# Later weight and input loads, one VectorE operation per tile for the block-diagonal keys, and retuned scheduling constants, in a two-layer sliding-window attention kernel

## The chip, the cores and the metric

The kernel runs on one core of a Trainium2 chip. The metric is the device time of the slowest core in microseconds, here simply of the one core. Executions of one kernel lie up to 1% or a little more apart (the kernel before took 368.29 to 371.98 us), so differences of 1% need several rounds. A run that is over 1.5% above the fastest of its kernel counts as slow; ratios leave it out. A ratio below is the mean time of one kernel's fast runs over that of the other's in the same rounds, so it is not quite the ratio of the medians that are quoted beside it. The kernel before stands at medians of 369.5 to 370.4 us, depending on the chip. A profile is one execution; its span is some 2 us shorter than the time.

## The reference

Two layers, with the same weights in both. In each, attention with a window of 256 over 2048 rows (32 heads of 16), and then a small MLP for the single row whose router value is highest:

```python
q, k, v = heads(layernorm(x) @ wqkv)                  # S = 2048, D = 512, H = 32, Dh = 16
scores = einsum("bhqd,bhkd->bhqk", q, k) * Dh ** -0.5
mask = (i - j >= 0) & (i - j < 256)
x = x + merge(softmax(where(mask, scores, -1e9)) @ v) @ wo
r = layernorm(x) @ w_r                                 # router; one row is chosen
y = (silu(x_sel @ w_gate) * (x_sel @ w_up)) @ w_down * sigmoid(r_sel)
x = layernorm(x) + scatter(y)
# ... both parts once more
```

## The kernel before

A program in Python lists every instruction of 32 tiles (16 of 128 rows, two layers) with its dependencies, an estimated duration and a priority. A list scheduler simulates the engines with those durations and from that fixes the order on each engine and the semaphores. So an instruction's estimated duration and a handful of priority constants decide the order of all the others. Each engine then works through its own list in that order (in `x8_late`, below, one instruction of VectorE's waits for 9.50 us, and everything behind it stands).

A tile's keys go from PSUM to `KTN`, and from there, block-diagonally for four heads, to `KT`: for each of four heads a multiplication by a 0/1 column of `KM`.

```python
def pk(MB=banks[1]):                                   # keys of one tile
    S.prio_base = p0 + self.P_K * 1e6 if L or m else -7e6
    ...                                                # 16 matmuls into the shared PSUM bank
    S.add("dve", lambda e: e.tensor_copy(out=self.KTN[:, k2], in_=...), dur=690, name="evk", tr=t)
    S.prio_base += self.P_KBD * 1e6 if L or m else 0.0
    for hh in range(4):
        S.add("dve", lambda e, hh=hh: e.tensor_scalar(
            out=self.KT[:, k4, :, :, hh, :].rearrange("p s b k -> p (s b) k"),
            in0=self.KTN[:, k2].rearrange("p s (b k) -> p (s b) k", k=32),
            scalar1=self.KM[:, hh:hh + 1], scalar2=None, op0=ALU.mult), dur=470, name="kbd", ...)
```

The query eviction to `QT` comes behind these on VectorE, and the output projection of the tile before waits for it, as keys, queries, values and output projection take turns in one PSUM bank.

A tile's values go from VectorE (`VN`) to DRAM (`vscr`) and come back spread out as `VBD` in four loads; only then can the product of probabilities and values (PV) run. GpSimd multiplies the probabilities by a mask (128x384), and makes the layer-norm of a tile two ahead: from VectorE's aggregate (`MV`) through a power (the reciprocal root) to `XN`. `XN` and the attention output `OT` are transposed by DMA. V writes, V loads, transposes and x loads are issued in one queue, SyncE's.

```python
ldx(0, 1, ...); ldw(1, ...); ldw(0, ...); ldx(1, 2, ...); ldw(2, ...)       # first two x tiles, wqkv
self.late_loads = [ldx(2, 4), lwo, lwr, ldx(4, 8), ldx(8, 16)]               # all after the first statistics
```

## Time and profile before

| | |
|---|---|
| time, median of 3 (lowest, highest) | 369.74 us (369.0, 370.61) |
| span of the profile, granted clock | 368.4 us, 0.969 |
| TensorE, VectorE, ScalarE, GpSimd busy | 92, 76, 73, 67% |

The rows of the page are read as: engine, operation, output<-inputs, shape, count, busy time and mean ns of one, idle time ahead of it.

### The profile page before, as it was taken

The page shows a single profiled execution, that of the slowest core. Times are in us where ns is not written, and L with a number is a line of the kernel's source. Part 1 is how long each engine was busy: PE and PEld are TensorE (multiplying, and loading weights), DVE is VectorE, ACT ScalarE, POOL GpSimd, SP SyncE. Part 2 cuts the span into 40 slices and gives each one's busy share as a digit, 9 for nine tenths or more (in the row PEclk, how much of TensorE's full clock was granted, in tenths as well). Part 3 has the DMA queues.
Part 4 walks back from the last instruction along what each step waited for, and adds up shares of the span by engine and source line. Part 5 has one row for each costly group of instructions (what it writes and reads, how often), then busy time and mean ns, then how long its engine had stood idle before and what let it go on. Part 6 is the DMA issues. An engine that isn't in the chain of part 4 may idle for free.

```text
span 368.4 us, 17614 instructions
## 1 busy us (share of the span) xinstructions
PE 339.3 (92%) x7770; PEld 274.3 (74%) x7770; DVE 281.0 (76%) x702; ACT 270.5 (73%) x296; POOL 245.5 (67%) x457
## 2 busy tenths in 40 slices
PE   8868889999999999999888998999999999999993
PEld 3566767888888888888677677877777788888771
DVE  7947768878888778777884597997787777786870
ACT  6559667888888888899191697779888888889600
POOL 4477758787877877766490479987776676566530
PEclk9969999999999999999997899999999999999986
DMA  8643524565555443363322123433232343322110
GB/s 261 229 73 63 115 63 113 134 123 124 104 102 103 84 118 93 88 99 91 89 59 21 30 48 78 60 64 74 52 72 61 77 77 76 77 58 56 27 32 25
DMA packets 72725, 31.25 MB, mean 85 GB/s; under 512 B 52672, under 2 KB 72000, under 8 KB 72640
## 3 DMA queue, kind: packets, MB, share of 16 engines
q1 hardware_dynamic: 70384, 27.81, 35.3%
q10 hardware_dynamic: 2256, 2.23, 1.9%
q8 instruction: 63, 1.03, 1.2%
q14 instruction: 22, 0.18, 0.2%
HBM read 14.29 MB, written 7.87 MB: 60 GB/s over the span
## 4 chain that ended last, share of the span: by engine, by line
PE 60%; DVE 21%; POOL 6%; DMA 5%; ACT 4%; issue 2%; DVEq 0%; POOLq 0%
PE f_PS L1331 16%; PE f_PS L1292 13%; PE f_PS L790 11%; PE f_PS L857 8%; DVE f_KT L816 8%; PE f_PS L826 6%; ACT f_PT L1301 4%; DMA f_OT<-f_ONORM 3%; POOL f_PT L1307 3%; DVE f_KTN L812 2%; DVE f_QT L1146 2%; PE f_PS L1010 2%; DMA f_XNT<-f_XN 1%; PE f_PS L1352 1%; DVE f_ST L744 1%
## 5 line engine op out<-in xcount | busy, mean ns | idle before, releaser
L1301 ACT ACTIVATE f_PT<-f_PS 128x1024 bf16<-128x1024 f32 x276 | 260.6, 1027 | 67.0 <-PE f_PS L1292 39.8
L1307 POOL TENSOR_TENSOR f_PT<-f_PT,f_TM 128x384 bf16<-128x384 bf16 x128 | 117.9, 922 | 39.1 <-ACT f_PT L1301 37.3
L1331 PEld LDWEIGHTS f_PS<-f_VBD,f_PT 128*128 128x128 bf16 x2880 | 106.2, 98 | 22.7 <-DVE f_ONORM L844 5.4
L1331 PE MATMUL f_PS<-f_VBD,f_PT 128*128 128x68 bf16 x2880 | 115.4, 197 | 5.2 <-POOL f_MV L748 2.8
L1292 PE MATMUL f_PS<-f_QT,f_KT 64*128 64x128 bf16 (+3 forms) x2976 | 90.2, 203 | 2.8 <-ACT f_PT L1301 2.4
L1292 PEld LDWEIGHTS f_PS<-f_QT,f_KT 64*128 64x128 bf16 x2976 | 70.4, 94 | 15.9 <-ACT f_PT L1301 5.5
L790 PE MATMUL f_PS<-f_XNT,f_wqkv 128*128 128x128 bf16 x1024 | 69.9, 223 | 2.3 <-DVE f_VN L829 0.9
L790 PEld LDWEIGHTS f_PS<-f_XNT,f_wqkv 128*128 128x128 bf16 x1024 | 59.8, 100 | 6.1 <-DVE f_VN L829 1.0
L816 DVE TENSOR_SCALAR f_KT<-f_KTN,f_KM 128x512 bf16<-128x512 bf16 x128 | 60.1, 529 | 1.0
L857 PE MATMUL f_PS<-f_wo,f_OT 128*128 128x512 bf16 x128 | 33.6, 384 | 9.5 <-DVE f_QT L1146 5.1
L812 DVE CAST f_KTN<-f_PS 128x512 bf16<-128x512 f32 x32 | 22.1, 690 | 26.0 <-PE f_PS L790 26.0
L880 POOL TENSOR_SCALAR f_RSM<-f_xres 128x1 f32<-128x1 f32 x32 | 7.6, 239 | 46.5 <-DVE f_xres L874 45.4
L826 PE MATMUL f_PS<-f_wqkv,f_XNT 128*128 128x512 bf16 x128 | 33.4, 381 | 0.8 <-DVE f_QT L1146 0.8
L844 DVE TENSOR_TENSOR f_ONORM<-f_PS,f_RDA 128x256 bf16<-128x256 f32 x64 | 27.0, 422 | 1.8
L875 DVE SCALAR_TENSOR_TENSOR f_JUNK<-f_xres,f_WR 128x512 bf16<-128x512 f32 x32 | 25.1, 784 | 0.1
L857 PEld LDWEIGHTS f_PS<-f_wo,f_OT 128*128 128x128 bf16 x128 | 10.1, 96 | 19.6 <-issue 6.9
L1290 PE MATMUL f_PS<-f_BM,f_II 64*128 64x64 bf16 (+1 forms) x256 | 24.6, 189 | 0.0
L829 DVE CAST f_VN<-f_PS 128x512 bf16<-128x512 f32 x32 | 22.1, 690 | 3.0 <-PE f_PS L826 2.5
L842 DVE RECIPROCAL f_RDA<-f_PS 128x16 f32<-128x16 f32 x64 | 16.1, 251 | 10.3 <-PE f_PS L1331 9.9
L1146 DVE CAST f_QT<-f_PS 128x512 bf16<-128x512 f32 x31 | 21.1, 681 | 3.5 <-PE f_PS L790 3.4
L873 DVE BATCH_NORM_STATS2 f_ST<-f_xres 128x6 f32<-128x512 f32 x32 | 22.2, 692 | 1.0
L882 POOL TENSOR_TENSOR f_xres<-f_RSM,f_MHALF 128x1 f32<-128x1 f32 x32 | 17.8, 555 | 6.8 <-DVE f_DOT L878 3.7
(133 smaller groups left out, 286.2 us busy)
## 6 DMA issues: line engine op xcount, KB each, us to landing
f_vscr<-f_VN SPq DMA_DIRECT2D x32, 136.0 KB, 2.0
f_VBD<-f_vscr SPq DMA_DIRECT2D x128, 34.0 KB, 2.4
out_dram<-f_OUTB SPq DMA_DIRECT2D x16, 128.0 KB, 2.6
f_xin<-in_B_w_down_dram SPq DMA_DIRECT2D x14, 128.0 KB, 2.1
f_wg<-in_B_w_gate_dram SPq DMA_DIRECT2D x7, 256.0 KB, 3.7
f_wu<-in_B_w_up_dram SPq DMA_DIRECT2D x7, 256.0 KB, 3.9
f_wqkv<-in_A_wqkv_dram ACTq DMA_DIRECT2D x3, 512.0 KB, 5.7
f_xscr<-f_xres SPq DMA_DIRECT2D x5, 256.0 KB, 2.3
```

The costliest lines, as they stand in the source:

```text
L790: r = e.matmul(self.bank(MB)[:, 128 * s:128 * s + 128], lhsT=self.wqkv[:, kc, off:off + 128], rhs=self.XNT[:, k2, kc, :], start=(kc == 0), ...
L812: S.add("dve", lambda e: e.tensor_copy(out=self.KTN[:, k2], in_=self.bank(MB)[:, 0:512].rearrange("p (s t) -> p s t", s=4)), reads=[], wri ...
L816: S.add("dve", lambda e, hh=hh: e.tensor_scalar(out=self.KT[:, k4, :, :, hh, :].rearrange("p s b k -> p (s b) k"), in0=self.KTN[:, k2].rea ...
L826: return e.matmul(self.bank(MB)[:, 0:512], lhsT=self.XNT[:, k2, kc, :], rhs=self.wqkv[:, kc, 1024:1536], start=(kc == 0), stop=(kc == 3))
L844: S.add("dve", lambda e: e.tensor_tensor(out=self.ONORM[:, ko, 256 * half:256 * half + 256].rearrange("p (h d) -> p h d", d=16), in0=acc[: ...
L857: return e.matmul(self.bank(MB)[:, 0:512], lhsT=self.OT[:, ko, kc, :], rhs=self.wo[:, kc, :], start=(kc == 0), stop=(kc == 3))
L875: S.add(D, lambda e: e.scalar_tensor_tensor(out=self.JUNK[:], in0=x, scalar=1.0, in1=self.WR16[:], op0=ALU.mult, op1=ALU.mult, accum_out=s ...
L1146: self.S.add("dve", lambda e: e.tensor_copy(out=self.QT[:, k2], in_=self.bank(MB)[:, 0:512].rearrange("p (s t) -> p s t", s=4)), reads=[], ...
L1292: r = e.matmul(o, lhsT=self.KT[p, (b // 4) % 4, s, b % 4].rearrange("p h k -> p (h k)"), rhs=self.QT[p, k2, s, q:q + w], start=(i == 0), s ...
L1301: S.add("act", lambda e: e.activation(out=view, in_=self.PS[:, b0:b0 + 2, 0:128 * nu].rearrange("p h (u c) -> p h u c", u=nu), func=ACTF.E ...
L1307: S.add("pool", lambda e: e.tensor_tensor(out=w, in0=w, in1=self.TM[:].unsqueeze(1).broadcast_to([128, k, 2, 32]), op=ALU.mult), reads=["t ...
L1331: r = e.matmul(self.bank(BK_PV)[:, c0:c0 + 68], lhsT=self.PT[:, w1:w1 + 128], rhs=self.VBD[:, (b // 4) % 4, b % 4].rearrange("p h (g c) -> ...
```

## The change

Its intent: keep the DMA engines free for the first tiles by sending the loads that are needed later, later; and write the four heads' keys by one instruction with a mask tensor, so that VectorE does less. The scheduler's constants were tuned again with it.

```diff
-        self.late_loads = [lambda d: ldx(2, 4, ...), lambda d: ldx(4, 8, ...), lambda d: ldx(8, 16, ...)]
+        self.late_loads = [(0, "st6_0", lambda d: ldx(2, 4, ...)), (0, "vn0", lambda d: ldx(4, 8, ...)),
+                           (1, "vn1", lambda d: ldx(8, 16, ...))]          # vn0, vn1: eviction of the first, second V tile
+        self.late_loads += [(0, "xnt0", lwo), (0, "vn0", lwr)]              # w_r now on SyncE's queue
...
-            for hh in range(4):
-                S.add("dve", lambda e, hh=hh: e.tensor_scalar(... scalar1=self.KM[:, hh:hh + 1] ...), dur=470, name="kbd")
+            S.add("dve", lambda e: e.tensor_tensor(
+                out=self.KT[:, k4].rearrange("p s b h k -> p (s b) h k"),
+                in0=self.KTN[:, k2].rearrange(...).unsqueeze(2).broadcast_to([128, 16, 4, 32]),
+                in1=self.KMB[:].unsqueeze(1).broadcast_to([128, 16, 4, 32]), op=ALU.mult), dur=1450, name="kbd")
...
-    P_Q = -0.321;  P_K = -0.417;  P_V = 0.232;  P_STEP = 1.112;  P_NORM = -0.33;   P_LEAD = 730.15
+    P_Q = -0.343;  P_K = -0.361;  P_V = 0.129;  P_STEP = 1.169;  P_NORM = -0.838;  P_LEAD = 456.083
     # cut: P_SP, P_PVJ, P_KBD, P_LN, P_FIN, P_MG, P_PV likewise
```

Below, **D** is the loads, **K** the key operation and **C** the constants. D also moves two small VectorE operations on w_r (`init_late`) behind the first tile's projections.

More of the change, by code (lines that the diff above doesn't have):

```diff
@@ L630, in alloc @@
         self.KM = self.sb("KM", [128, 4], F32)
+        self.KMB = self.sb("KMB", [128, 4, 32], BF16)
         self.IDXI = self.sb("IDXI", [128, NT], I32)
@@ L686, in init @@
         ldw(2, -8.7e9)
-        self.late_loads = [lambda d: ldx(2, 4, "sp", -8.6e9, d), lambda d: ldx(4, 8, "sp", -8.3e9, d), lambda d: ldx(8, 16, "sp", -8.2e9, d)]
+        self.late_loads = [(0, "st6_0", lambda d: ldx(2, 4, "sp", -8.6e9, d)), (0, "vn0", lambda d: ldx(4, 8, "sp", -4.9e6, d)),
+                           (1, "vn1", lambda d: ldx(8, 16, "sp", -4.7e6, d))]
         def lwo(d):
             S.dma("act", lambda e: e.dma_start(self.wo[:], self.A_wo.rearrange("(kc p) n -> p kc n", p=128)),
-                  writes=["wo"], nbytes=1440000, name="ld_wo", dur=650, prio=-8.5e9, extra_deps=d)
+                  writes=["wo"], nbytes=1440000, name="ld_wo", dur=650, prio=-6.8e6, extra_deps=d)
         def lwr(d):
-            S.dma("act", lambda e: e.dma_start(self.WR16[:], self.B_w_r.partition_broadcast(128)),
-                  writes=["wr16"], nbytes=1540000, name="ld_wr", dur=650, prio=-8.4e9, extra_deps=d)
-        self.late_loads.insert(1, lwo)
-        self.late_loads.insert(2, lwr)
+            S.dma("sp", lambda e: e.dma_start(self.WR16[:], self.B_w_r.partition_broadcast(128)),
+                  writes=["wr16"], nbytes=1540000, name="ld_wr", dur=650, prio=-4.8e6, extra_deps=d)
+        self.late_loads += [(0, "xnt0", lwo), (0, "vn0", lwr)]
         S.add(P, lambda e: e.memset(self.MHALF[:], -0.5), writes=["mhalf"], dur=100, prio=-9.5e9)
@@ L714, in init @@
                   reads=["kf2"], writes=["km%d" % hh], dur=150)
+        S.add(D, lambda e: e.tensor_copy(out=self.KMB[:], in_=self.KM[:].unsqueeze(2).broadcast_to([128, 4, 32])), reads=["km%d" % hh for hh in range(4)], writes=["kmb"], dur=200)
         S.add(P, lambda e: e.memset(self.ONESF[:], 1.0), writes=["onesf"], dur=200, prio=-8.1e9)
@@ L814, in pk @@
             S.prio_base += self.P_KBD * 1e6 if L or m else 0.0
-            for hh in range(4):
-                S.add("dve", lambda e, hh=hh: e.tensor_scalar(
-                    out=self.KT[:, k4, :, :, hh, :].rearrange("p s b k -> p (s b) k"),
-                    in0=self.KTN[:, k2].rearrange("p s (b k) -> p (s b) k", k=32), scalar1=self.KM[:, hh:hh + 1], scalar2=None, op0=ALU.mult),
-                    reads=["ktn%d" % k2, "km%d" % hh], writes=["kt%d_%d" % (k4, hh)], dur=470, name="kbd")
+            S.add("dve", lambda e: e.tensor_tensor(
+                out=self.KT[:, k4].rearrange("p s b h k -> p (s b) h k"),
+                in0=self.KTN[:, k2].rearrange("p s (b k) -> p (s b) k", k=32).unsqueeze(2).broadcast_to([128, 16, 4, 32]),
+                in1=self.KMB[:].unsqueeze(1).broadcast_to([128, 16, 4, 32]), op=ALU.mult),
+                reads=["ktn%d" % k2, "kmb"], writes=["kt%d_%d" % (k4, hh) for hh in range(4)], dur=1450, name="kbd")
         def pv(MB=banks[2]):
@@ L835, in proj @@
             f()
+        if L == 0 and m < 2:
+            for i, k, f in self.late_loads:
+                if i == m:
+                    f([S.last_writer[k]])
+            if m == 0:
+                S.prio_base = 0.0
+                self.init_late()
     def norm_half(self, L, m, half):
@@ L1095, in start @@
     def start(self):
-        for f in self.late_loads:
-            f([self.S.last_writer["st6_0"]])
-        self.init_late()
         self.S.prio_base = 0.0
@@ L1105 @@
     RING = 10
-    P_Q = -0.321
-    P_K = -0.417
-    P_V = 0.232
-    P_STEP = 1.112
-    P_NORM = -0.33
-    P_LEAD = 730.15
+    P_Q = -0.343
+    P_K = -0.361
+    P_V = 0.129
+    P_STEP = 1.169
+    P_NORM = -0.838
+    P_LEAD = 456.083
     VISIT = 3
-    P_SP = 1.267
+    P_SP = 1.137
     P_MLP = ((1, 1, 7), (1, 2, 4))
-    P_PVJ = [0.815, 0.0, -0.041, 0.091, -0.285, 0.0, 0.078, -0.469, 0.0]
-    P_KBD = 0.191
+    P_PVJ = [0.815, 0.0, -0.113, 0.015, -0.285, 0.0, 0.347, -0.723, 0.0]
+    P_KBD = 0.452
     P_EV = 0.0
-    P_LN = -2.482
+    P_LN = -2.273
     P_PRJ = -1.035
-    P_FIN = 1.533
-    P_MG = -0.485
-    P_PV = 0.741
+    P_FIN = 2.046
+    P_MG = -0.741
+    P_PV = 0.807
     warm0 = 26
```

## The prediction

> **What bounds the kernel now.** I read the page first (busy shares, granted clock), then busy time by stage, then the waits of TensorE, then the timelines around the two places that the change touches. The page's totals, and busy time of each engine in four stretches (start:end, length, then busy us and number of instructions per engine, granted clock, DMA share, GB/s):
>
> ```profile
> span 368.4 us, 17614 instructions
> PE 339.3 (92%) x7770; PEld 274.3 (74%) x7770; DVE 281.0 (76%) x702; ACT 270.5 (73%) x296; POOL 245.5 (67%) x457
> ...
> 12.00:34.00 22.00, 16.30 (x332) 13.17 (x331) 14.83 (x38) 13.72 (x15) 16.14 (x30) 0.84 0.46 106
> 34.00:60.00 26.00, 22.17 (x522) 18.12 (x520) 20.53 (x51) 17.68 (x19) 18.34 (x36) 1.00 0.42 102
> 60.00:176.00 116.00, 114.47 (x2825) 96.12 (x2822) 93.21 (x216) 99.01 (x106) 87.95 (x158) 1.00 0.50 104
> ...
> 240.00:332.00 92.00, 88.83 (x2166) 73.38 (x2166) 73.01 (x160) 76.59 (x83) 62.62 (x112) 1.00 0.31 69
> ```
>
> TensorE carries the kernel from 60 us on: 114.5 of 116 us busy in layer 0, 88.8 of 92 in layer 1. The start is another matter: from 12 to 60 us it is busy for 38.5 of 48 us and runs part of that at a reduced clock. So there are two sorts of gain to be had, in the start, where TensorE stands, and in the small gaps of layer 1. In a steady tile nothing but TensorE's own work is left: the output projections of the last steady tiles start at 311.40, 321.25 and 331.10, so 9.85 us a tile, against 10.23 to 10.29 where a gap is left (260.58, 270.81, 281.10, 291.32).
>
> The gap of the start, from the timelines of the DMA queue, of TensorE and of VectorE (start, length, what, idle before and its releaser):
>
> ```profile
> 12.41 0.34 SPq L1341 DMA_DIRECT2D f_vscr<-f_VN  x1
> 17.16 1.75 SPq L1344 DMA_DIRECT2D f_VBD<-f_vscr  x4
> ...
> 21.92 1.06 PE L1331 MATMUL f_PS<-f_VBD,f_PT 128*128 128x68 bf16 x16 [2.80 <-POOL f_MV L748]
> 22.79 1.90 PE L790 MATMUL f_PS<-f_XNT,f_wqkv 128*128 128x128 bf16 x16
> ...
> 15.34 1.07 PE L790 MATMUL f_PS<-f_XNT,f_wqkv 128*128 128x128 bf16 x16 [0.86 <-DVE f_SWC L735]
> 17.20 1.04 PE L826 MATMUL f_PS<-f_wqkv,f_XNT 128*128 128x512 bf16 x4 [0.79 <-DVE f_QT L1146]
> ```
>
> The first V tile goes to DRAM and comes back spread out. The write is issued at 12.41, the loads back only at 17.16: 4.75 us, while the same write lands in 2.3 us in the median. The mean rate of the first 12 us is 264 GB/s, and all inputs of these first loads (x 2 MB, wqkv 1.5 MB, wo 0.5 MB, w_r 0.13 MB) are issued by 6.4 us: 4.1 MB at 264 GB/s is 15.6 us, so the V write stands behind them. The wait is put down to GpSimd, but the instruction waits for the four loads as well, and those are what came last. The same 16 key matmuls take 1.90 us after that gap against 1.07 us before it.
>
> The gap of layer 1, one tile (VectorE, GpSimd, TensorE):
>
> ```profile
> 10.44 1.14 DVE L816 TENSOR_SCALAR f_KT<-f_KTN,f_KM 128x512 bf16<-128x512 bf16 x4
> 267.69 2.38 DVE L816 TENSOR_SCALAR f_KT<-f_KTN,f_KM 128x512 bf16<-128x512 bf16 x4
> ...
> 267.19 0.92 POOL L1307 TENSOR_TENSOR f_PT<-f_PT,f_TM 128x384 bf16<-128x384 bf16 x1
> 268.10 0.91 POOL L758 TENSOR_SCALAR f_XN<-f_xres,f_MV 128x512 bf16<-128x512 f32 x1
> 268.97 0.94 POOL L1307 TENSOR_TENSOR f_PT<-f_PT,f_TM 128x384 bf16<-128x384 bf16 x1
> ...
> 270.81 1.02 PE L857 MATMUL f_PS<-f_wo,f_OT 128*128 128x512 bf16 x4 [0.47 <-DVE f_QT L1146]
> ```
>
> The four key writes take 1.14 us with GpSimd idle and 2.38 us with it at work: between two of them a GpSimd instruction gets in. Behind them stands the query eviction, behind it the output projection (all share one PSUM bank), and TensorE stands 0.47 us.
>
> [...]
>
> **The change part by part.**
>
> (1) Loads. Still early are x tiles 0 to 3 and wqkv, 2 MB; wo waits for the first transposed tile (8.4 us), x tiles 4 to 7 and w_r are issued right after the first V write, x 8 to 15 after the second. What is issued before the V write is 2.5 MB, at 264 GB/s 9.5 us, so done at about 11 us, and the write at 12.4 finds the DMA engines nearly empty. I take the median landing, 2.3 us instead of 4.75: 2.4 us sooner. The 0.64 MB issued behind it (2.4 us at that rate) can delay the loads back a little; I count that under the range. With TensorE's gap before the first PV down from 2.8 to under 1 us I expect the clock to hold: of the 3.4 us of full clock lost from 20 to 30 us I count 2.0. The order of the instructions also shows that the sum over w_r leaves VectorE's queue ahead of the second tile's key eviction, and that the second V projection moves behind three more score groups: of the waits of 0.86 and 0.79 us I count 1.0. From 34 to 60 us, in which TensorE idles 3.8 us, I count 0.6 for tiles that run earlier and for transposes that no longer stand behind the 256 KB scratch store in the queue. Sum of the start: 2.4 + 2.0 + 1.0 + 0.6 = 6.0 us.
>
> (2) Keys. Taken away are 128 tensor_scalars (60.1 us busy, 529 ns each), added 32 tensor_tensors of 2048 elements [...] and one 0.2 us mask copy in the set-up. [...] TensorE's waits for that eviction sum to 1.0 us from 62 to 175, 1.2 from 175 to 240 and 3.1 from 240 to 345 us; I count 0.8, 1.0 and 2.8, together 4.6 us. The rest of VectorE's saving lies beside TensorE and is worth nothing.
>
> (3) Scheduling constants. In the order of TensorE's instructions the steady tiles are the same, step for step; the first five tiles, the layer boundary and the last two tiles differ. I count 0.
>
> Sum 6.0 + 4.6 = 10.6 us; 369.7 - 10.6 = 359.1. I add 1 us [...]: **360 us**.
>
> **Rivals.** (a) [...] 2048 elements take about 2.2 us (estimate: 4 x 512 elements at the 0.69 us of a 512-element eviction, less fixed cost). Then (2) gives nothing and GpSimd, [...] makes the attention masks late: 365 us. [...] (b) GpSimd becomes the late one[...]. For: it is busy 9.5 to 9.8 of 10 us from 220 to 240 us. Against: from 240 to 332 it is 62.6 of 92 us busy, so some 3 us a tile are free. That costs 1 to 3 us at the layer boundary: 362. (c) The start is bound by something else: exp, the transposes or x tiles 4 to 7, now late, take the place of the V round trip, and half of the 6 us stays: 363. For: TensorE also waited 1.9 us there for attention-output transposes. (d) More comes than I count: 12 to 60 us holds 9.5 us of idle and 3.5 us of lost clock; with two thirds recovered, 357.
>
> **Range and chances.** (a) and (c) together put the top near 366, (d) the bottom near 355. The 2% line is 362.3 us, 2.3 above my figure, at a spread of some 4 us: faster by over 2% 0.70, within 2% 0.29, slower 0.01.
>
> **What will show it.** In the profile after: first PV matmul before 20 us rather than at 21.92, no gap of 2 us before it, granted clock above 0.9 from 20 to 30 us; [...] TensorE's waits for the query eviction near 0 and a 9.85 us tile throughout layer 1. I am wrong if the key op takes 2 us or more, if the first PV is still after 21 us, or if the layer boundary (176 to 240 us) has grown by over 2 us.

## More of the kernel before

The prediction shows the lines that I read. Two more of the kernel before will be needed: the shares of the chain that ended last, and the group of GpSimd's masks.

```profile
PE 60%; DVE 21%; POOL 6%; DMA 5%; ACT 4%; issue 2%; DVEq 0%; POOLq 0%
...
L1307 POOL TENSOR_TENSOR f_PT<-f_PT,f_TM 128x384 bf16<-128x384 bf16 x128 | 117.9, 922 | 39.1 <-ACT f_PT L1301 37.3
```

GpSimd is on that chain for 6%, and a mask takes 922 ns.

## The result, and the profile after

The changed kernel takes **374.36 us** (373.63 to 375.3, 4 runs) against 370.12 us for the kernel before on the same chip. The ratio is 1.012, with a 95% interval of 1.0084 to 1.0156: within 2%, but slower, and 14 us from my figure of 360. The profiled span went from 368.4 to 371.9 us.

The page after: span, chain, masks, key operation.

```profile
span 371.9 us, 17514 instructions
...
PE 45%; POOL 28%; DVE 17%; DMA 5%; issue 2%; SPq 1%; ACT 1%; DVEq 0%; POOLq 0%
...
L1313 POOL TENSOR_TENSOR f_PT<-f_PT,f_TM 128x384 bf16<-128x384 bf16 x128 | 134.6, 1057 | 26.9 <-ACT f_PT L1307 25.2
...
L817 DVE TENSOR_TENSOR f_KT<-f_KTN,f_KMB 128x2048 bf16<-128x2048 bf16 x32 | 45.5, 1420 | 0.9
```

VectorE's key writes fell from 60.1 to 45.5 us. But GpSimd's share of the chain went from 6 to 28%, and a mask from 922 to 1057 ns. The stretches of the prediction again (start:end, length, busy us and count for TensorE, its weight loads, VectorE, ScalarE, GpSimd, then granted clock, DMA share, GB/s):

```profile
12.00:34.00 22.00, 13.60 (x324) 10.66 (x323) 13.52 (x27) 13.88 (x15) 15.05 (x24) 0.98 0.50 128
34.00:60.00 26.00, 23.12 (x541) 19.34 (x540) 21.13 (x42) 18.12 (x20) 21.00 (x38) 0.95 0.41 82
60.00:176.00 116.00, 110.66 (x2693) 90.61 (x2686) 87.29 (x178) 94.98 (x101) 92.85 (x154) 1.00 0.45 105
...
240.00:332.00 92.00, 89.36 (x2193) 73.62 (x2193) 67.37 (x137) 77.43 (x84) 74.87 (x123) 1.00 0.39 70
```

Layer 0, where I had counted on 0.8 us of gain, lost: TensorE is busy 110.7 of 116 us and was 114.5. Layer 1 won a little.

**The start**, from the timelines of the DMA queue and of TensorE after the change:

```profile
12.54 0.34 SPq L1347 DMA_DIRECT2D f_vscr<-f_VN  x1
...
14.33 2.78 SPq L1350 DMA_DIRECT2D f_VBD<-f_vscr  x4
...
22.30 0.57 SPq L677 DMA_DIRECT2D f_xin<-in_A_x_dram  x1
22.92 0.57 SPq L1347 DMA_DIRECT2D f_vscr<-f_VN  x1
...
28.86 2.26 SPq L1350 DMA_DIRECT2D f_VBD<-f_vscr  x4
...
19.43 0.68 PE L1337 MATMUL f_PS<-f_VBD,f_PT 128*128 128x68 bf16 x16
...
32.94 1.97 PE L1337 MATMUL f_PS<-f_VBD,f_PT 128*128 128x68 bf16 x32 [3.20 <-DMA f_VBD<-f_vscr]
```

The first V write is back for loading after 1.79 us (14.33 less 12.54; it was 4.75) and the first PV runs at 19.43 us without a gap: this is what was predicted. But the 1 MB load of x tiles 8 to 15 is issued at 22.30, right ahead of the second V write at 22.92, and that one takes 5.94 us. TensorE stands 3.20 us at 32.94, and gets half clock (a granted clock of 0.5) for 3.41 us. In this profile the wait was not removed; it went one tile on.

**A tile of layer 0**, first before, then after (timelines of VectorE, GpSimd and TensorE; the two show the same place of the tile):

```profile
105.04 0.92 POOL L1307 TENSOR_TENSOR f_PT<-f_PT,f_TM 128x384 bf16<-128x384 bf16 x1
...
105.34 1.93 DVE L816 TENSOR_SCALAR f_KT<-f_KTN,f_KM 128x512 bf16<-128x512 bf16 x4
...
107.58 0.26 POOL L756 TENSOR_SCALAR f_MV<-f_MV 128x1 f32<-128x1 f32 x1
...
108.20 0.12 DVE L745 BATCH_NORM_AGGREGATE f_MV<-f_ST 128x2 f32<-128x6 f32 x1
108.32 0.42 DVE L844 TENSOR_TENSOR f_ONORM<-f_PS,f_RDA 128x256 bf16<-128x256 f32 x1
...
108.99 0.75 PE L1331 MATMUL f_PS<-f_VBD,f_PT 128*128 128x68 bf16 x18
```

```profile
98.43 1.48 DVE L817 TENSOR_TENSOR f_KT<-f_KTN,f_KMB 128x2048 bf16<-128x2048 bf16 x1
...
98.81 1.88 POOL L1313 TENSOR_TENSOR f_PT<-f_PT,f_TM 128x384 bf16<-128x384 bf16 x1
...
102.17 0.26 POOL L758 TENSOR_SCALAR f_MV<-f_MV 128x1 f32<-128x1 f32 x1
...
102.46 0.18 DVE L747 BATCH_NORM_AGGREGATE f_MV<-f_ST 128x2 f32<-128x6 f32 x1 [1.08 <-POOL f_MV L758]
102.56 0.39 DVE L853 TENSOR_TENSOR f_ONORM<-f_PS,f_RDA 128x256 bf16<-128x256 f32 x1
...
103.01 0.76 PE L1337 MATMUL f_PS<-f_VBD,f_PT 128*128 128x68 bf16 x18 [1.06 <-DVE f_ONORM L853]
```

Read the second fence from the top. The mask that starts while the key operation runs takes 1.88 us and not 0.92. It is no single case: counted over the whole traces, the 19 masks that start while a key operation runs take 1.85 us in the mean, and the 98 that do not overlap one take 0.92; in the kernel before, the 21 that start under the four writes take 0.95. GpSimd's layer-norm (three more instructions behind it) is therefore later, and its last part ends 4.00 us after the key operation began (102.17 + 0.26 - 98.43); before it was 2.50 us (107.58 + 0.26 - 105.34). VectorE's queue has an aggregate of 0.18 us for a later tile, which may overwrite `MV` only then, **ahead of** the normalization that TensorE needs. In the kernel before the same two stand in the same order, and the aggregate never waits; where it stands right ahead of a normalization, between 60 and 176 us, it starts 0.09 to 0.36 us after GpSimd's last part has ended. Now it waits 1.08 us, and TensorE 1.06 us behind it. The waits of TensorE's matmuls for the normalization come to 3.5 us between 82 and 158 us; before there were none.

**Layer 1.** TensorE's largest waits from 240 to 345 us (who waits <- for whom: us in total, times, longest), before and after:

```profile
PE f_PS L857 <- DVE f_QT L1146: 3.1, 6, 0.7
```

```profile
PE f_PS L792 <- DVE f_VN L831: 1.1, 2, 0.7
```

The wait for the query eviction, which the prediction was after here, is gone.

### The profile page after: what moved, and what is told of

Its sections match the earlier page's. It is cut to its first block, busy times and chain, and to the rows that moved or that the text cites. A ratio compares the mean times of both kernels' runs of the same rounds, so it can differ in the third digit from the quotient of the medians.

```text
span 371.9 us, 17514 instructions
## 1 busy us (share of the span) xinstructions
PE 336.1 (90%) x7770; PEld 270.5 (73%) x7770; DVE 268.0 (72%) x607; ACT 271.1 (73%) x296; POOL 265.8 (71%) x457
## 4 chain that ended last, share of the span: by engine, by line
PE 45%; POOL 28%; DVE 17%; DMA 5%; issue 2%; SPq 1%; ACT 1%; DVEq 0%; POOLq 0%
PE f_PS L1337 13%; POOL f_PT L1313 12%; PE f_PS L1298 10%; PE f_PS L792 8%; PE f_PS L828 4%; PE f_PS L866 4%; POOL f_XN L760 4%; POOL f_MV L750 3%; POOL f_xres L901 3%; DVE f_JUNK L884 2%; POOL f_xres L891 2%; DVE f_ST L882 2%; DVE f_xres L870 2%; DVE f_ST L746 2%; DVE f_VN L831 2%
## 5 line engine op out<-in xcount | busy, mean ns | idle before, releaser
L1313 POOL TENSOR_TENSOR f_PT<-f_PT,f_TM 128x384 bf16<-128x384 bf16 x128 | 134.6, 1057 | 26.9 <-ACT f_PT L1307 25.2
L1337 PEld LDWEIGHTS f_PS<-f_VBD,f_PT 128*128 128x128 bf16 x2880 | 105.1, 98 | 30.2 <-DVE f_ONORM L853 13.0
L792 PE MATMUL f_PS<-f_XNT,f_wqkv 128*128 128x128 bf16 x1024 | 68.3, 220 | 6.7 <-DVE f_KTN L814 2.5
L792 PEld LDWEIGHTS f_PS<-f_XNT,f_wqkv 128*128 128x128 bf16 x1024 | 58.4, 98 | 10.8 <-DVE f_KTN L814 3.2
L817 DVE TENSOR_TENSOR f_KT<-f_KTN,f_KMB 128x2048 bf16<-128x2048 bf16 x32 | 45.5, 1420 | 0.9
L750 POOL TENSOR_TENSOR f_MV<-f_MV,f_MHALF 128x1 f32<-128x1 f32 x32 | 18.4, 579 | 1.5
```

The lines of the kernel that those rows point to most:

```text
L750: S.add("pool", lambda e: e.tensor_tensor(out=MV[:, k2, 3:4], in0=MV[:, k2, 2:3], in1=self.MHALF[:], op=ALU.pow), reads=["mhalf", "mvb%d" ...
L792: r = e.matmul(self.bank(MB)[:, 128 * s:128 * s + 128], lhsT=self.wqkv[:, kc, off:off + 128], rhs=self.XNT[:, k2, kc, :], start=(kc == 0), ...
L817: S.add("dve", lambda e: e.tensor_tensor(out=self.KT[:, k4].rearrange("p s b h k -> p (s b) h k"), in0=self.KTN[:, k2].rearrange("p s (b k ...
L1313: S.add("pool", lambda e: e.tensor_tensor(out=w, in0=w, in1=self.TM[:].unsqueeze(1).broadcast_to([128, k, 2, 32]), op=ALU.mult), reads=["t ...
L1337: r = e.matmul(self.bank(BK_PV)[:, c0:c0 + 68], lhsT=self.PT[:, w1:w1 + 128], rhs=self.VBD[:, (b // 4) % 4, b % 4].rearrange("p h (g c) -> ...
```

## The experiments

Busy time and spans do not show where time goes, as the executions shift against each other. I therefore count work. In steady tiles, where TensorE's order is the same in most of these kernels, I count exponentials: each kernel runs the same 276 on ScalarE, 138 a layer. The table has the start of the n-th, counted from 0, in the profile of the kernel before, and for the others how much later (+) or earlier (-) it is. The 60th lies in tile 7 and the 120th starts tile 14 of layer 0, the 138th starts layer 1, the 192nd lies in its tile 6 (tiles are counted from 0 too).

| | before, us | after | tt_in_before_order | four_in_after_order | c_only | no_k | no_d | tt_layer1 | c_tt_late | cd_tt_late |
|---|---|---|---|---|---|---|---|---|---|---|
| 60th | 90.22 | +3.1 | +2.1 | +4.1 | -1.3 | +2.2 | -0.6 | -0.8 | -3.6 | -0.7 |
| 120th | 156.84 | +5.0 | +3.3 | +4.0 | -1.3 | +2.2 | +1.4 | +0.1 | -3.6 | -0.7 |
| 192nd | 254.16 | +6.5 | +6.7 | +5.6 | +0.3 | +3.2 | +3.8 | +3.3 | -1.0 | +1.1 |
| 264th | 334.94 | +3.9 | +3.8 | +5.4 | +0.1 | +3.0 | +1.4 | +0.8 | -3.9 | -1.5 |
| end | 368.44 | +3.5 | +4.5 | +5.0 | -0.4 | +2.6 | +1.3 | +1.1 | -3.4 | -0.7 |

In the first tiles the orders differ, and a kernel can be ahead in exponentials and behind in projections. There I count matmuls of all kinds, in the profiles that have all 7770 (start of the n-th, counted from 0, us):

| matmul | before | no_d | after | x8_spread | c_tt_late | cd_tt_late |
|---|---|---|---|---|---|---|
| 300th | 28.47 | 25.55 | 25.07 | 24.75 | 24.12 | 25.52 |
| 600th | 44.03 | 40.38 | 44.06 | 38.65 | 40.64 | 41.19 |
| 900th | 58.65 | 56.08 | 59.36 | 55.87 | 53.77 | 54.35 |
| 1500th | 83.57 | 83.06 | 86.72 | 83.11 | 79.61 | 82.35 |

Two cautions. The start of one and the same order varies between executions: up to the 144th exponential `c_only` and `c_tt_late` have the same instructions in the same order, but for the copy that makes the mask tensor, and differ by 2.4 us at the 60th. And half clock (a granted clock of 0.5) came in stretches of 3.41, 6.83 or 10.24 us: at the layer boundary it lasted 6.83 us in the profiles of before, after and `no_k`, and 10.24 us in those of `c_only`, `no_d`, `tt_in_before_order`, `four_in_after_order` and `tt_layer1` (a granted clock of 0.57 from 198 to 206 us before, of 0.57 from 197 to 209 us in `tt_layer1`); 3.41 us more at half clock are 1.7 us of full clock. What rests on a microsecond or two of the start or of the boundary rests on the ratios, not on these tables.

### The parts, each alone and each left out

My theory was that K did it (theory 1), the rivals that C (theory 2) or D (theory 3) did. The edits are the three parts of the diff above, put into the kernel before or taken out of the changed one.

`k_only`, before + K:

> The kernel before with one part of the change: the four key writes become one tensor_tensor with the mask tensor; loads and constants stay. Theory 1 ([...] VectorE's queue then waits for GpSimd ahead of the normalization that TensorE needs): the loss is here, 373 to 375 us against 370.1, with masks of some 1050 ns instead of 922 and TensorE waiting over 3 us for the normalized output in layer 0. Theory 2 (the retuned constants made the loss, the key op is a small gain): 367 to 370 us. Theory 3 (the loads made it): 367 to 370 us as well.

`d_only`, before + D:

> The kernel before with one part of the change: the reordered loads; key writes and constants stay. Theory 1: the start neither wins nor loses more than 1 us, so 369 to 371 us, as the wait for the V round trip moves from the first tile (first PV before 20 us) to a later one, behind the 1 MB load of x tiles 8 to 15. Theory 3 (the loads made the loss): 373 us or more. My prediction's step 1 would have it at 364 us.

`c_only`, before + C:

> The kernel before with only the retuned priority constants. Theory 1: 369 to 371 us (the constants alone do little; steady tiles have the same TensorE order). Theory 2: 373 us or more, that is the whole loss.

`no_k`, after - K:

> The changed kernel with the four key writes put back (reordered loads and new constants stay). Theory 1: the loss of layer 0 goes and the gain of layer 1 too, 369 to 371 us, masks back near 920 ns. Theories 2 and 3: still 373 us or more.

`no_d`, after - D (run later):

> The changed kernel with the old loads (all issued by 6.4 us); the new key operation and the new constants stay. With four key writes and the new constants, the reordered loads cost 3.6 us by the 48th exponential (373.3 against 368.3 us). If loads and key operation do not depend on each other, this is 369 to 371.5 us, 3 to 5 below the changed kernel's 374.4. If the loads are worth their predicted gain next to the new key operation, it is slower than 374.4.

| | D | K | C | median us | ratio to before (95%) |
|---|---|---|---|---|---|
| c_only | | | x | 368.25 | 0.9927 (0.9900 to 0.9955) |
| d_only | x | | | 382.0 | 1.0279 (1.0227 to 1.0331) |
| k_only | | x | | 402.67 | 1.0843 (1.0792 to 1.0893) |
| no_k | x | | x | 373.27 | 1.0023 (0.9942 to 1.0103) |
| no_d | | x | x | 371.49 | 1.006 (1.0026 to 1.0094) |
| after | x | x | x | 374.36 | 1.012 (1.0084 to 1.0156) |

(The profiled run of `d_only` was slow; only its order and its fast runs are used. One run of `no_k` was slow too. The medians are over all runs, the ratios over fast ones. D with K and the old constants was not run.)

No theory had expected this. K alone costs not 4 but 32 us, D alone not 0 but 10 (its fast runs), and C, which I had counted as 0, wins 0.7% alone and takes nearly all of those losses back. The parts are not independent, and the reason is the scheduler. The order of TensorE's instructions in steady tiles of layer 0, one tile of the kernel before (in every second one the V projection stands some PV matmuls later) and two of `k_only` (number of matmuls; S scores, PV, V, KQ and O projections; the trace of `k_only` lacks some records, filled in here):

```
before:  PV18 S34 V4 PV30 S32 KQ16 PV36 KQ16 S38 PV12 O4
k_only:  PV40 KQ16 PV8 S32 KQ16 S38 V4 PV36 O4  |  PV12 S34 KQ16 PV48 S32 KQ16 PV36 S38 V4 PV12 S34 O4
```

The changed kernel has the first pattern again. One operation of 1450 ns by estimate in place of four of 470, or loads that are estimated to land later, and the list scheduler falls into another pattern, in which projections that share a PSUM bank follow one another closely. With the new constants it is back. **So an experiment that puts one part into such a kernel measures mostly the order.** The parts had to be tried again with the order held fixed.

### K with the order held

After the scheduler has run, the four key writes are replaced where the last of them stands, and every other instruction keeps its place; I compared the lists of all engines, and they differ in nothing else (but for the copy that makes the mask tensor).

```diff
+def fold(S):                       # after S.schedule()
+    for g in groups_of_four(kbd):
+        k = last of g in VectorE's order
+        k.fn = one tensor_tensor;  k.deps |= deps of g;  the others of g emit nothing
```

> The kernel before with the one tensor_tensor put where the last of the four key writes stood, after the scheduler has run: the order of every other instruction on every engine stays word for word, so this prices the operation alone, where the run with the new op and a new order took 402.7 us. Theory 2 (the order is what cost 32 us there; the operation itself is a small gain): 366 to 370 us, with the 3 us of waits for the query eviction in layer 1 gone. Theory 1 [...]: 372 us or more.

And the reverse, four writes emitted by one entry of the changed kernel's order:

```diff
-            S.add("dve", lambda e: e.tensor_tensor(...), dur=1450, name="kbd")
+            S.add("dve", four, dur=1450, name="kbd")      # four() issues the four tensor_scalars
```

> The changed kernel with four tensor_scalars emitted where the one tensor_tensor stands, all else in the same order. Theory 1: the waits of TensorE for the normalized output in layer 0 (3.8 us) go, those for the query eviction in layer 1 (3.1 us) come back, 372 to 375 us against 374.4. Theory 2 (order): layer 0 stays as slow as in the changed kernel and layer 1 loses 3 us more: 376 to 378 us.

`tt_in_before_order`: 373.36 us, ratio 1.0064 (1.0020 to 1.0108). `four_in_after_order`: 373.70 us, 1.0056 (0.9994 to 1.0118). In the old order the operation alone so costs 0.6%, clear of noise. In the new order the difference to after (1.012) is 0.6% as well, but the two were run in different calls, their intervals overlap, and the medians differ by 0.7 us: there the times alone do not show it. K in the old order takes 373.36 us, which is 29 us less than the 402.67 us in the order that K brought about. With C in place and the order free, K costs more: 0.9927 to 1.0060 from `c_only` to `no_d`, 1.0023 to 1.012 from `no_k` to after.

The waits from 82 to 158 us, in layer 0, of `tt_in_before_order` (TensorE's first line, then one of VectorE's), and of `four_in_after_order` (TensorE's first line):

```profile
PE f_PS L1339 <- DVE f_ONORM L852: 2.6, 4, 1.1
...
DVE f_MV L747 <- POOL f_MV L758: 5.2, 6, 1.1
```

```profile
PE f_PS L867 <- DVE f_QT L1153: 1.0, 4, 0.3
```

And GpSimd's masks in the two, `tt_in_before_order` first:

```profile
L1315 POOL TENSOR_TENSOR f_PT<-f_PT,f_TM 128x384 bf16<-128x384 bf16 x128 | 130.9, 1025 | 27.8 <-ACT f_PT L1309 25.6
```

```profile
L1314 POOL TENSOR_TENSOR f_PT<-f_PT,f_TM 128x384 bf16<-128x384 bf16 x128 | 117.8, 924 | 42.0 <-ACT f_PT L1308 40.7
```

With the operation in, the masks take 1025 ns and not 924, VectorE's aggregate waits for GpSimd and TensorE for the normalization; with it out, in the changed kernel's own order, both lists have no such line. That shows theory 1's chain of waits; how much of the 0.6% it makes up is not shown by it. By the table, K in the old order loses 1.2 us from the 60th to the 120th exponential and wins 2.9 from the 192nd to the 264th. In the new order it loses 1.9 us from the 60th to the 120th, where four writes win 0.1, and it wins 2.6 us from the 192nd to the 264th, where four writes win 0.1. K's gain in layer 1 is what was predicted (2.8 us). Its loss elsewhere was not.

### What makes GpSimd late, and what stands behind it

`onorm_first`: in the changed kernel's order of VectorE, four aggregates change places with the normalization right behind them.

```diff
+        if b is a normalization and a, right ahead of it, is the aggregate of mv0 or mv1:
+            q[p], q[p + 1] = q[p + 1], q[p]
```

> The changed kernel with four swaps in VectorE's order: a layer-norm aggregate that waits for GpSimd goes behind the normalization that stands right after it. If VectorE's queue standing at that aggregate is what makes TensorE wait four times 0.5 to 1.06 us in layer 0, 3 us are won: 371 to 372 us. If GpSimd's own lateness is what counts, the waits move to the masks and nothing is won: 374 us.

373.57 us, ratio 1.008 (1.0027 to 1.0133), against 1.012 (1.0084 to 1.0156) for the changed kernel. It was run at another time. The waits for the normalization at those places fell (one of 0.73 us is left of four), but two of 0.7 us for the residual sum, which is further back in VectorE's queue, came up in their place. From the 60th to the 96th exponential this kernel lost 0.2 us on the kernel before, the changed kernel 1.1; but to the 120th it lost 1.3, the changed kernel 1.9. Neither expectation fits: the queue order is part of the waits, other waits on VectorE take their place, and the intervals of the times overlap.

`tt_halves`: the key operation as two of half the length, in the old order, so that GpSimd can get in between. The 373 us in the expectation are for the case that only the sum of the two counts.

```diff
-                return e.tensor_tensor(out=..., in0=..., in1=...)                 # 2048 elements
+                for a in (0, 8):
+                    r = e.tensor_tensor(out=...[:, a:a + 8], in0=...[:, a:a + 8], in1=...)   # 1024 each
```

> The kernel before, same order everywhere, with two tensor_tensors of half the size (1024 elements) in place of the four key writes of each tile, against 373.4 us with one of 2048. If [...] a mask can get in after 0.6 us and not after 1.2 us: masks below 1000 ns, the waits for the normalized output in layer 0 fall from 2.6 us (82 to 158 us) to below 1 us, and the time to 369 to 371 us. [...] 373 us as before.

```profile
L1317 POOL TENSOR_TENSOR f_PT<-f_PT,f_TM 128x384 bf16<-128x384 bf16 x128 | 123.5, 967 | 29.4 <-ACT f_PT L1311 27.2
```

The mask fell to 967 ns from 1025, and the waits for the normalization from 2.6 to 0.4 us, as expected if a mask gets in between the halves. The time did not: 373.1 us, ratio 1.0083 (1.0026 to 1.0140). A half took 896 ns, so the pair takes 1.79 us against 1.40 for the one, and waits of 2.1 us for transposes of the attention output and 1.5 us for VectorE's reciprocal came instead. The shorter operation makes the masks less late; the pair costs VectorE 0.39 us a tile more, and other waits on it come up. So this run does not show what the waits for the normalization cost by themselves.

### K by stage

`tt_layer1`: the kernel before, same order, K from the third tile of layer 1 on.

```diff
-    for a in range(0, len(ids), 4):
+    for a in range(4 * 18, len(ids), 4):
```

> The kernel before, same order everywhere, with the tensor_tensor only from the third tile of layer 1 on. With it in all tiles, layer 0 lost 3.3 us, the boundary 3.4 and layer 1 won 2.9 us. If these add up by stage, only the gain is left: 366.5 to 368 us against 370.0, with the stage up to the boundary as in the kernel before. If the operation's loss is anywhere else, 369.5 us or more.

371.05 us, ratio 1.0017 (0.9954 to 1.0080): my expectation of 366.5 to 368 us was missed. Layer 0 is as before (+0.1 at the 120th exponential), and from the 192nd to the 264th it wins 2.6 us. But it reaches the 192nd at +3.3 us. Of that, +1.2 us came between the 144th and the 156th, with 10.24 us of half clock for 6.83, and 1.7 us from the 156th to the 192nd, in the first tiles of layer 1. There the operation seems to lose as in layer 0. `c_tt_late`, below, tests that and doesn't settle it.

### D: which load holds what

`x8_late`: the changed kernel with the 1 MB load moved behind the V loads of the third tile; only SyncE's list changes.

```diff
+    q.remove(load of x 8 to 15);  q.insert(q.index(last V load of tile 2) + 1, load of x 8 to 15)
```

> The changed kernel with one load moved in its queue: x tiles 8 to 15 (1 MB) are issued behind the V loads of the third tile and not right ahead of the second V write. If that load is what holds the second V tile (5.9 us between its write and its loads), TensorE's wait of 3.2 us at 33 us and the half clock behind it go: 370 to 372 us against 374.4. If something else comes due there at the same time (exp, the transposes), less than 1 us is won: 373.5 us or more.

Slower: 381.81 us, ratio 1.0321 (1.0271 to 1.0371). The timelines of the DMA queue and of VectorE:

```profile
24.50 2.01 SPq L1350 DMA_DIRECT2D f_VBD<-f_vscr  x4
...
42.12 1.29 DVE L746 BATCH_NORM_STATS2 f_ST<-f_xin 128x6 f32<-128x512 bf16 x2 [9.50 <-DMA f_xin<-in_A_x_dram]
```

The V loads of the second tile did come at 24.50 and not 28.86 us, so the load was what held them. But the test was bad: the scheduler had put the statistics of tile 8 early in VectorE's list, and everything behind them stood for 9.50 us.

`x8_mid`: the same load behind the V loads of the second tile, so that it lands in time for those statistics.

```diff
-    v = [o.idx for o in S.ops if o.name == "vld"][11]
+    v = [o.idx for o in S.ops if o.name == "vld"][7]
```

> The changed kernel with x tiles 8 to 15 issued right behind the V loads of the second tile. The run with the load behind the third tile brought the second tile's V loads from 28.86 to 24.50 us, but VectorE then stood 9.5 us at a statistics instruction for x tile 8, which is early in its order, so that run was a bad test. Here the load should land by 31 to 32 us, about when VectorE gets to it. If the load is what moved the V wait to the second tile, the wait of 3.2 us at 33 us and the half clock behind it go, and the kernel takes 370 to 372 us against 374.4. If VectorE stands again for x tile 8, or another wait comes due, 373 us or more.

372.2 us, ratio 1.0038 (0.9961 to 1.0115): better by the middle of the interval, but the intervals overlap. The wait of 3.20 us for the second V tile is gone. The third V tile is now the one behind the load:

```profile
30.97 0.34 SPq L1347 DMA_DIRECT2D f_vscr<-f_VN  x1
...
35.74 2.43 SPq L1350 DMA_DIRECT2D f_VBD<-f_vscr  x4
```

Its write takes 4.77 us to come back, the issue of a transpose between the two 2.34 us, and TensorE waits 1.74 us at 34.66 with half clock for 6.83 us. So the V write behind the load is the slow one again. But the wait at 34.66 is not for it, as its loads are issued only at 35.74; the profile names no releaser for that wait, and its cause stays open. TensorE's one wait for V loads up to 66 us is 0.74 us, at 54.98.

`x8_spread`: in the changed kernel, three loads of 256, 256 and 512 KB behind the V loads of three tiles. `cd_tt_late`: the same with four key writes up to the fifth tile of layer 1 and K after.

```diff
-                           (1, "vn1", lambda d: ldx(8, 16, ...))]
+                           (1, "vb1_3", lambda d: ldx(8, 10, ...)), (2, "vb2_3", lambda d: ldx(10, 12, ...)),
+                           (3, "vb3_3", lambda d: ldx(12, 16, ...))]
```

> The changed kernel with x tiles 8 to 15 in three loads (256, 256 and 512 KB), each behind the V loads of a tile (the second, third and fourth) in place of one load of 1 MB. A few instructions of tiles 3 to 9 change place, as the scheduler has two loads more. If it is the lump that holds the V round trip behind it, the gaps between V write and V loads stay below 3.5 us in tiles 2 to 4 (5.9 in the changed kernel in the second, 4.8 in the third with the load in one piece behind it), no wait for V above 1.5 us is left, and the time is 369.5 to 372 us. If the round trip is slow there for another reason, waits of 3 us stay and the time is 373 us or more.

> As the run before, but with the reordered loads, x tiles 8 to 15 spread over three loads. If the start gain of 3 us is then kept: 363 to 365 us. If the reordered loads cost something whatever the cut: 367 us or more.

In the profile of `x8_spread` the V round trips of tiles 2 to 4 take 2.44, 1.76 and 2.07 us, no wait for V is left, and the whole of what the loads cost in the start is back: 38.65 us at the 600th matmul against 44.06 after the change, 83.11 at the 1500th, as in `no_d`. So it was the lump, as expected. But the time is not: 375.92 us, ratio 1.0169 (1.0140 to 1.0198), worse than the changed kernel. The profiled run, at 373.75 us, was the fastest of four, and the orders of tiles 3 to 9 differ a little, so this run is not clean, and where its slower executions lose stays open. That removing the wait wins time is therefore not shown. In `cd_tt_late`, 368.69 us, ratio 0.9952 (0.9908 to 0.9995), one place could be of the kind. The last load, 512 KB, is issued at 50.35 us, and then (queue, TensorE):

```profile
52.69 2.73 SPq L769 DMA_TRANSPOSE f_OT<-f_ONORM  x1
...
57.23 0.60 PE L873 MATMUL f_PS<-f_wo,f_OT 128*128 128x512 bf16 x2 [1.95 <-DMA f_OT<-f_ONORM]
```

This transpose issue, the second behind the load, takes 2.73 us against 1.20 to 1.25 for the three before it, and TensorE waits 1.95 us for its result. That the load does it is not shown: `no_d` has a transpose issue of 2.34 us at 53.45, with no x load near.

**What D costs** can be read three times with C in place: `c_only` to `no_k` 0.9927 to 1.0023, `no_d` to after 1.006 to 1.012, `c_tt_late` (below) to `cd_tt_late` 0.9896 to 0.9952. It is 0.6 to 1.0%, 2 to 4 us, each time against the change. (The intervals of each pair overlap a little, and `no_d` and after come from different calls; it is the three together that carry this. In the first and the last pair the order changes with the loads, and `cd_tt_late` has the spread loads.) From `no_d` to after the table of matmuls says where: 0.5 us won at the 300th, 3.7 us lost at the 600th (3.20 us of wait for the second V tile and its half clock), and the same 3.7 us at the 1500th. And it says that most of the 3.4 us by which the changed kernel leads the kernel before at the 300th matmul does not come from the loads: `no_d`, with the old loads, leads by 2.9. Its first V tile takes 5.63 us, its first PV runs at 22.14 us, and TensorE still waits only 1.27 us for it, as the new order has other work to put there.

### A kernel faster than both

`c_tt_layer1`: old loads, new constants, the order of `c_only`, K from the third tile of layer 1 on. `c_tt_late`: from the sixth tile on.

> A try at a kernel that beats both: the old loads, the new constants with the order that they give to four key writes (368.2 us), and the tensor_tensor only from the third tile of layer 1 on. If the parts add up: 365 to 366.5 us against 370.0 before and 374.4 after.

> Old loads, new constants, four key writes up to the fifth tile of layer 1 and the tensor_tensor from the sixth on, same order as with four writes everywhere (368.2 us; 366.6 us with the tensor_tensor from the third tile on). If the operation loses in the first tiles of layer 1, where GpSimd is busy over 90%, and gains 2.6 us after them: 365 to 366.5 us, and no loss between the 156th and 192nd exponential. If it makes no difference where in layer 1 it starts: 366.5 to 367.5 us.

366.62 us, ratio 0.9922 (0.9856 to 0.9988), and **366.31 us, ratio 0.9896 (0.9866 to 0.9926)**. The second beats the kernel before by 1% and the changed one by 2% (over different calls), and has the old loads and K only where it wins. From the 192nd to the 264th exponential it wins 2.8 us on the kernel before, `c_only` 0.2. Its expectation held in the time but not in "no loss between the 156th and 192nd": it loses 0.9 us there, `c_tt_layer1` 1.6 and `c_only` 0.5. Whether the first tiles of layer 1 should keep four writes stays open: the two intervals overlap, and `c_only` at 0.9927 (0.9900 to 0.9955) overlaps with both.

## Why the prediction was wrong, point by point

**Step (1), loads, 6.0 us: wrong.** What it says of the transfer held: in the profile before, the last x load landed at 16.77 us, the V write at 17.14 and the last of the four V loads at 21.58, just ahead of the first PV at 21.92. After the change the V write came back in 1.79 us rather than 4.75, the first PV was at 19.43 us (predicted: before 20), and the granted clock from 12 to 34 us was 0.98 (it was 0.84, with half clock from 21.04 to 27.87 us, which began in the wait of 2.80 us). Three things in the step failed. Its terms "2.4 + 2.0 + 1.0" took a sooner first PV for a gain of as much; against `no_d`, the same kernel with the old loads, it was worth 0.5 us at the 300th matmul, as the order can put other work there. And it priced only the transfers *ahead* of the first V write. "x 8 to 15 after the second" stands in it with no price, though 1 MB at the rate that I used myself (264 GB/s) is 4 us, and took 6.0 us to land, in which the second V tile's write, its loads and two transposes are wanted. It is also misread: the load waits for the eviction of the second V tile, not for its write, and was issued 0.62 us ahead of that write (22.30 against 22.92). The second round trip took 5.94 us and cost 3.7 us. In the kernel before, the large loads run while the engines have little work yet (70 matmuls in the first 12 us, against 2825 in the 116 us of layer 0), and delay one V tile (4.75 us from write to loads); moved, they delay a later one (5.94 us) that has no slack either. Three comparisons put D at a loss of 0.6 to 1.0%.

That the second V tile's wait is what makes this loss is shown in single profiles alone; the time did not come back where the wait was removed (`x8_mid`, `x8_spread`). One reading was off as well: "2.3 us in the median" is the median of V writes and V loads together; the page has 2.0 us for the write alone.

**Step (2), keys, 4.6 us: right in one term of three.** The operation took 1.19 us at the least and 1.42 in the mean, so rival (a), which had it at 2.2 us, is refuted. (Those 2.2 us are near four evictions at 0.69 us less three times the 0.16 us that VectorE's aggregate of two values takes in the same profile.) That the operation would be short enough to end the waits for the query eviction was my estimate. The step's term for layer 1, 2.8 us, measured 2.6 to 2.9 us, and the last steady tiles there take 9.72 us each (predicted 9.85). The terms for layer 0 (+0.8) and the boundary (+1.0) had the wrong sign: with the order held, 1.2 us were lost from the 60th to the 120th exponential and 3.4 more by the 192nd, of which 1.7 can be a piece of half clock. In sum K costs 0.6%; predicted was a gain of 4.6 us, 1.2%. The step that failed is "The rest of VectorE's saving lies beside TensorE and is worth nothing", together with the 1 us added for GpSimd: I followed the longer instruction as far as the query eviction, and not through GpSimd, whose masks took 1.85 us for 0.92 where they started under it, back to VectorE.

**Rival (b)** named the right engine and the wrong place. Its place was the layer boundary, and its argument against itself that GpSimd has some 3 us a tile free in layer 1. That was true and beside the point: in layer 0, at 88 of 116 us busy, GpSimd is not full either. What counts is the one chain mask, layer-norm, `MV`, VectorE's aggregate, normalization, PV, which had 0.09 to 0.36 us to spare. I had looked for the gaps on the engine at its limit and then at what it waits for; that finds the gaps that are there. The gap of layer 0 was not there before the change. To see it coming one has to ask of each instruction that becomes later what waits for it, and how long that already waits.

**Step (3), constants, 0: wrong**, and it hid the rest. That steady tiles have the same order after the change as before was taken to mean that the constants do nothing. They do 0.7% alone, and without them K takes 402.67 us. Equal orders were their result.

**What was to show it wrong** did not: the key operation below 2 us, the first PV before 21 us, and 1.6 us more from the 120th to the 192nd exponential. None of these looked at layer 0 or at the second V tile.

**The range** of 355 to 366 us rested on rivals (a) and (c) together. By their own figures (365 and 363 against 360) they add up to 8 us, which is 368 and not "near 366"; the result lies above that too. Two terms with the wrong sign were not among its cases.

## What to carry to other kernels

- When a large transfer is moved out of one wait, name the transfers that will be behind it at its new place and whether they have slack. In this kernel the load in one piece slowed the V write behind it at the planned place and at one other (5.94 and 4.77 us), and in a third it came too late for an instruction that needed it (9.50 us).
- When one long instruction replaces several short ones, look at which instructions of other engines get longer while it runs (here GpSimd's masks, 1.85 us for 0.92), and follow the ones behind them to whoever waits for them. The instruction that pays can be one that the change doesn't touch, because it stands in a queue behind one that waits.
- Where a scheduler decides the order, a part of a change can't be priced by putting it in alone; hold the order and swap the operation.
